# Earlier x slabs, a constant tile for the dummy matmuls, and one product moved from GpSimd to VectorE

## The chip, the cores and the metric

The kernel runs on one core of a Trainium2 chip. The metric is the device time of that core in microseconds (us), the median of several executions; most executions of one kernel agree within 0.3%. Engines are named as in the profile: PE (TensorE matmul), PEld (its weight load), DVE (VectorE), ACT (ScalarE), POOL (GpSimd), SP (SyncE, which issues most transfers here).

Each run sets a kernel against the kernel before, on the same chip and in the same rounds. A ratio is the mean time of the one kernel's fast runs over the mean of the other's fast runs of the same rounds, so it is not quite the ratio of the medians quoted beside it; the bracket after it is a 95% interval.

## The reference, cut to what matters

```python
x  = A_x                                    # 2048 x 640, bf16
xn = layernorm(x)
s  = irfft2(rfft2(xn) * (w_r + 1j*w_i))     # spectral branch
h  = gelu(xn @ w_gate) * (xn @ w_up)        # 640 -> 1536
g  = silu(h @ w_down)                       # 1536 -> 640
return x + s * g
```

## The kernel before

x is held as 16 slabs of 128 x 640. The first two gate/up tiles ("early") multiply **raw** x, so that the PE needn't wait for the layernorm. Their outputs are corrected later on VectorE: out = (raw + wsum * b) * a, where the rows a and b of all four slabs go through DRAM once and come back broadcast as RB. The layernorm statistics of a slab are made on VectorE or on ScalarE in two passes. Normalized slabs are transposed for gate and up, and pairs of them are folded and sent through a small matmul ("fold") for the spectral branch, copied out of PSUM, and stored to DRAM from buffers `mc`.

All work is a list of tasks; a small planner inside the kernel orders each engine's instructions from estimated costs and ranks. Any change of a cost or a rank may therefore reorder everything. Buffers are rings: `mc` has two, `th` two, `ge` three.

```python
    BUFS = dict(sp=2, pg=2, pu=2, s1=4, ma=2, mb=2, mc=2, ..., ge=3, th=2, ...)
    ...
    load_w(Wg, gv, g_in, 0, 2, land=4690)       # slab 0 is issued from ScalarE before this
    load_x(1, 2, land=5200)
    load_w(Wu, uv, u_in, 0, 2, land=6790)
    load_x(2, 3, land=7280)
    load_x(3, 4, land=7750)
    ...
    # stats on ScalarE: its scratch tile is of the ring "th"
    nc.scalar.activation(out=place(junk, (D,)), in_=x, func=ACT.Copy, ...)
    ...
    # the rows a, b: also in a "th" buffer, held until they are stored to DRAM
    sr, rt = Slot("sp"), Slot("th")
    ...
    rs = dma(D5, lambda: rt.tile[0:8, :], (0, -5, 0), 4096, ...)
    rb_in = dma(RB..., D5...partition_broadcast(P), (0, -5, 1), 524288, after=[rs])
    ...
    # the correction of an early tile; k = 0 gate, 1 up
    out = copy of PSUM to ev
    m = scalar_tensor_tensor(ev = RB[:, 1] * WSUM + ev)      # VectorE
    normed.append(... tensor_tensor(ev = ev * RB[:, 0]) on ("POOL" if k else "DVE"))
```

Of the kernel before, what the change touches and what calls it, by code (L numbers as in the profile page):

```python
# [12 lines left out]
BF16 = mybir.dt.bfloat16  # L13
ACT = mybir.ActivationFunctionType
ALU = mybir.AluOpType
P = 128
# [98 lines left out]
class Plan:  # L115
# [12 lines left out]
    def add(self, emit, eng, cost, rank, after=(), new=(), use=(), size=0, slow=1.0, hold=0, order=(), lag=0, land=0):  # L128
        engs = eng if isinstance(eng, dict) else {eng: cost}
        t = Task(emit=emit, engs=engs, rank=rank, after=list(after), new=list(new), size=size, slow=slow, hold=hold, order=list(order), lag=lag, land=land,  # L130
                 seq=len(self.tasks))
        for s in (*new, *use):
            s.users.append(t)
        self.tasks.append(t)
        return t
# [77 lines left out]
def c_act(n, psum=True, extra=0):  # L213
    return 0.833 * n + 60 + extra, 0.833 * n + 200 + extra
# [8 lines left out]
def kernel(  # L223
# [64 lines left out]
    def place(slot, shape, dt=BF16):  # L288
        if slot.tag in ("sp", "pg", "pu"):
            slot.tile = psum.tile([P, *shape], dt, tag=slot.tag, name=slot.tag)  # L290
        else:
            slot.tile = work.tile([P, *shape], dt, tag=slot.tag, name=slot.tag, bufs=BUFS[slot.tag])
        return slot.tile
# [22 lines left out]
    def load_x(a, b, land=0):  # L316
        seq[0] += 1
        t = dma(X[:, a:b, :], xv[:, a:b, :], (0, -4, seq[0]), (b - a) * 163840, use=[sX], land=land)
        for n in range(a, b):
            x_in[n] = t  # L320
# [9 lines left out]
    def load_w(sb, view, got, a, b, land=0):  # L330
        cs = slice(a * P, b * P)
        seq[0] += 1
        w = dma(sb[:, :, cs], view[:, :, cs], (0, -4, seq[0]), (b - a) * 163840, slow=1.1, land=land)
        for t in range(a, b):
            got[t] = w
# [19 lines left out]
    nc.scalar.activation(out=warm, in_=warm, func=ACT.Gelu_apprx_tanh)  # L355
    for w in WF:
        nc.gpsimd.memset(w[:, :, :, L:LP], 0.0)
    idle, heat = Slot("uT"), Slot("sp")

    def blank(e):  # L360
        nc.vector.memset(place(idle, (512,)), 0.0)

    def keep_warm(n, after, rank=(0, -9), ns=425):
        def go(e):
            if heat.tile is None:
                place(heat, (2, 512))
            for k in range(n):
                nc.tensor.matmul(heat.tile[:, k % 2, :], lhsT=idle.tile[:, 0:P], rhs=idle.tile,
                                 start=True, stop=True, skip_group_check=True)
        return add(go, "PE", (n * ns, n * ns), rank, after=after, new=[] if heat.users else [heat], use=[idle] + ([heat] if heat.users else []))  # L370
    seq[0] += 1
    x_in[0] = add(lambda e: None, "SP", (1, 1), (0, -5), size=1, land=3620)
    load_w(Wg, gv, g_in, 0, 2, land=4690)
    load_x(1, 2, land=5200)
    load_w(Wu, uv, u_in, 0, 2, land=6790)
    load_x(2, 3, land=7280)
    load_x(3, 4, land=7750)
    t = add(blank, "DVE", (330, 400), (0, -9), new=[idle])
    t = warmed = keep_warm(6, [t])
    load_gu(2, 4)  # L380
    load_x(4, 6)
    load_tab("f1")
# [71 lines left out]
    def turn_raw(n1):  # L454
        pt = Slot("sp")

        def half():
            return pt.tile[:, 0, :].bitcast(BF16)[:, 0:D]

        def mm(e):  # L460
            place(pt, (2, 512))
            for c in range(5):
                nc.tensor.transpose(out=half()[:, c * P:c * P + P], in_=X[:, n1, c * P:c * P + P], identity=ident)
        a = add(mm, "PE", c_pe(*[140] * 5), (0, n1), after=[x_in[n1], warmed], new=[pt], use=[sX])
        if n1 == 0:
            keep_warm(2, [a], (0, 0, 0))
        raw[n1] = add(lambda e: copy_on(e, XR[:, :, n1 * P + (n1 > 0):(n1 + 1) * P + (n1 > 0)], half().rearrange("p (c n) -> p c n", c=5)),
                      {"ACT": c_act(640)} if n1 < 2 else {"ACT": c_act(640), "DVE": (415, 560)}, None, (0, n1), after=[a], use=[pt], hold={1: 1000}.get(n1, 200))
    for n1 in range(4):
        turn_raw(n1)  # L470

# [68 lines left out]
            outs.append(add(cp, either(640), None, (1, 2 * j + s), after=[a] + outs, new=[] if s else [A], use=[pa, A] if s else [pa]))  # L540
        stored[j] = dma(lambda: D2[:, 2 * j:2 * j + 2, :], lambda: A.tile, (0, -1, j), 327680, after=outs, use=[A], slow=1.1)

    lead = ("DVE", "ACT", "DVE", "ACT")
    for n1 in range(NSLAB):
        if n1 % 2 == 0:
            xn_of[n1 // 2] = Slot("s1")
# [325 lines left out]
    def gate_up(grp, t):  # L872
        pg, pu, ge, u = Slot("pg"), Slot("pu"), Slot("ge"), Slot("uT")
        uT[grp, t] = u
        last = {}
        early = grp == 0 and t < 2
        for k, (w, ps, wt) in enumerate(((Wg, pg, g_in[t]), (Wu, pu, u_in[t]))):
            parts = [(128 * j, 128 * j + 128) for j in range(4)] if grp == 0 and t < 3 else [(0, 512)]
            mm = []
            for lo, hi in parts:  # L880
                def go(e, w=w, ps=ps, lo=lo, hi=hi):
                    if lo == 0:
                        place(ps, (512,))
                    for c in range(5):
                        more = early and lo == 0
                        nc.tensor.matmul(ps.tile[:, lo:hi + more], lhsT=w[:, c, t * P:(t + 1) * P],  # L886
                                         rhs=XR[:, c, lo + (lo > 0):hi + 1 if lo or more else hi] if early else xnT[:, c, grp * 512 + lo:grp * 512 + hi], start=(c == 0), stop=(c == 4),
                                         skip_group_check=True)
                step[0] += 1
                rk = (1, step[0]) if len(parts) == 1 else (0, 5, lo, k, t) if early else (1, lo // 128, t)  # L890
                got = raw if early else turned
                mm.append(add(go, "PE", c_pe(*[hi - lo] * 5), rk,
                              after=[wt] + mm[-2:] + [got[n] for n in range((grp * 512 + lo) // P, (grp * 512 + hi) // P)],
                              new=[ps] if lo == 0 else [], use=[] if lo == 0 else [ps]))
                if early and lo == 0:
                    sums_out[k, t] = add(lambda e, k=k, ps=ps: copy_on(e, WSUM[:, 2 * k + t:2 * k + t + 1], ps.tile[:, 128:129]),
                                         {"DVE": c_dve(1, 1, True)}, None, (0, -1), after=[mm[-1]], use=[ps])
                    mm.append(sums_out[k, t])
            last[id(w)] = mm[-1]

        def act(e, src=None):
            place(ge, (512,))
            nc.scalar.activation(out=ge.tile, in_=pg.tile if src is None else src, func=ACT.Gelu_apprx_tanh)  # L903

        def mul(e, src=None):
            place(u, (512,))
            nc.vector.tensor_tensor(out=u.tile, in0=pu.tile if src is None else src, in1=ge.tile, op=ALU.mult)  # L907
        if not early:
            a = add(act, "ACT", c_act(512), (0, step[0]), after=[last[id(Wg)]], new=[ge], use=[pg])
            u_done[grp, t] = add(mul, "DVE", c_dve(512, 1, True), (0, step[0]), after=[a, last[id(Wu)]], new=[u], use=[pu, ge])  # L910
            return
        normed, evs = [], []

        def four(s):
            return s.tile.rearrange("p (n t) -> p n t", n=4)
        for k, (w, ps) in enumerate(((Wg, pg), (Wu, pu))):
            ev = Slot(("IU", "R")[k])
            evs.append(ev)
            out = add(lambda e, ev=ev, ps=ps: copy_on(e, place(ev, (512,), FP32), ps.tile), {"ACT": c_act(512), "DVE": c_dve(512, 1, True)}, None, (1, 3, 0.5), after=[last[id(w)]], new=[ev], use=[ps])
            m = add(lambda e, ev=ev, k=k: nc.vector.scalar_tensor_tensor(out=four(ev), in0=RB[:, 1], scalar=WSUM[:, 2 * k + t:2 * k + t + 1], in1=four(ev),  # L920
                                                                         op0=ALU.mult, op1=ALU.add), "DVE", c_dve(512, 1), (0, 100), after=[out, rb_in, sums_out[k, t]], use=[ev])
            normed.append(add(lambda e, ev=ev: (nc.gpsimd if e == "POOL" else nc.vector).tensor_tensor(out=four(ev), in0=four(ev), in1=RB[:, 0], op=ALU.mult), *(("POOL", (1700, 1800), (1, 8)) if k else ("DVE", c_dve(512, 1), (0, 100))), after=[m], use=[ev]))
        a = add(lambda e: act(e, evs[0].tile), "ACT", c_act(512), (0, 100), after=normed[:1], new=[ge], use=evs[:1])
        u_done[grp, t] = add(lambda e: mul(e, evs[1].tile), "DVE", c_dve(512, 1), (0, 100), after=[a, normed[1]], new=[u], use=[ge, evs[1]])

# [127 lines left out]
```

## Time and profile before

| what | before |
|---|---|
| median of the first 3 runs | 202.65 us (202.62 to 202.78) |
| span of the profiled execution | 201.1 us |
| first gate matmul | 5.59 us |
| first gate matmul of 512 columns | 14.23 us |
| start of the last matmul group | 196.34 us |
| from there to the end | 4.74 us |

The first table of the page (engine, busy us, share of the span, instructions):

```profile
PE 195.2 (97%) x1527; PEld 117.4 (58%) x1527; DVE 149.7 (74%) x320; ACT 127.2 (63%) x224; POOL 33.1 (16%) x73
```

The PE is the bound, and the prediction below reads its stages, waits (what waited <- for what: us in all, times, longest) and head. The first is from the list of waits (what waited <- for what: us in all, times, longest), the second from the timeline of VectorE (start, length, instruction, idle time before it):

```profile
ACT mc L296 <- DMA D<-mc: 1.0, 1, 1.0
```

```profile
29.71 0.75 DVE L920 SCALAR_TENSOR_TENSOR IU<-RB,WSUM,IU 128x512 f32<-128x512 f32 x1 [1.12 <-DMA RB<-D]
```

ScalarE waits once, for 1.0 us, until a fold buffer `mc` has been stored. And the corrections start at 29.71, not when the PE or VectorE is ready, but when the rows RB are back from DRAM.

### The profile page before, as it was taken

The page shows a single profiled execution, that of the slowest core. Times are in us where ns is not written, and L with a number is a line of the kernel's source. Part 1 is how long each engine was busy: PE and PEld are TensorE (multiplying, and loading weights), DVE is VectorE, ACT ScalarE, POOL GpSimd, SP SyncE. Part 2 cuts the span into 40 slices and gives each one's busy share as a digit, 9 for nine tenths or more (in the row PEclk, how much of TensorE's full clock was granted, in tenths as well). Part 3 has the DMA queues.
Part 4 walks back from the last instruction along what each step waited for, and adds up shares of the span by engine and source line. Part 5 has one row for each costly group of instructions (what it writes and reads, how often), then busy time and mean ns, then how long its engine had stood idle before and what let it go on. Part 6 is the DMA issues. An engine that isn't in the chain of part 4 may idle for free.

```text
span 201.1 us, 4125 instructions
## 1 busy us (share of the span) xinstructions
PE 195.2 (97%) x1527; PEld 117.4 (58%) x1527; DVE 149.7 (74%) x320; ACT 127.2 (63%) x224; POOL 33.1 (16%) x73
## 2 busy tenths in 40 slices
PE   7999999999999999999999999999999999999992
PEld 2994444566544555677755555467765555457781
DVE  3789969999323249999998999933257788887774
ACT  3898997974632768778775766333466565766421
POOL 2412347596000000000000000000004122211210
PEclk9999999999999999999999999999999999999999
DMA  6999999569949677333244210117704332332432
GB/s 175 329 316 325 344 392 235 126 165 196 301 128 375 223 202 178 103 93 115 61 126 126 75 50 16 68 49 221 317 3 135 96 132 100 98 107 92 130 103 65
DMA packets 35894, 32.62 MB, mean 162 GB/s; under 512 B 10910, under 2 KB 32930, under 8 KB 35874
## 3 DMA queue, kind: packets, MB, share of 16 engines
q1 hardware_dynamic: 34434, 29.49, 49.1%
q0 software_dynamic: 1152, 2.66, 4.8%
q10 hardware_dynamic: 288, 0.20, 0.5%
q8 instruction: 12, 0.20, 0.4%
q14 instruction: 8, 0.07, 0.1%
HBM read 22.51 MB, written 9.19 MB: 158 GB/s over the span
## 4 chain that ended last, share of the span: by engine, by line
PE 79%; DMA 10%; SPq 4%; DVE 3%; issue 1%; ACT 1%; DVEq 0%
PE pg L886 19%; PE pu L886 19%; PE pg L970 13%; PE pu L970 12%; DMA X<-in_A_x_dram 6%; SPq L303 4%; DMA RB<-D 4%; PE sp L697 3%; PE sp L830 3%; PE sp L772 2%; PE sp L806 2%; PE sp L670 2%; PE sp L532 1%; PE sp L690 1%; PE sp L824 1%
## 5 line engine op out<-in xcount | busy, mean ns | idle before, releaser
L886 PE MATMUL pu<-xnT,Wu 128*128 128x512 bf16 (+1 forms) x245 | 57.6, 366 | 0.0
L886 PE MATMUL pg<-xnT,Wg 128*128 128x512 bf16 (+1 forms) x245 | 57.5, 366 | 0.0
L907 DVE TENSOR_TENSOR uT<-pu,ge 128x512 bf16<-128x512 f32 x46 | 31.7, 689 | 20.9 <-PE pu L886 18.4
L970 PEld LDWEIGHTS <-uT 128*128 128x128 bf16 x396 | 37.8, 98 | 14.1 <-issue 0.6
L903 ACT ACTIVATE ge<-pg 128x512 bf16<-128x512 f32 x46 | 27.4, 597 | 25.5 <-PE pg L886 25.0
L886 PEld LDWEIGHTS <-Wg 128*128 128x128 bf16 x285 | 25.2, 98 | 22.1
L886 PEld LDWEIGHTS <-Wu 128*128 128x128 bf16 x285 | 25.1, 98 | 21.8
L970 PE MATMUL pg<-Wd,uT 128*128 128x320 bf16 (+2 forms) x204 | 30.5, 293 | 0.4 <-ACT ge L903 0.4
L970 PE MATMUL pu<-Wd,uT 128*128 128x320 bf16 (+1 forms) x192 | 29.7, 297 | 0.0
L296 ACT CAST ma<-sp 128x644 bf16<-128x644 f32 (+1 forms) x32 | 23.4, 792 | 9.7 <-PE sp L830 7.9
L932 POOL COPY xr<-s 1x1 bf16<-1x1 bf16 x1 | 0.2, 182 | 101.8 <-DVE s L856 101.8
L933 POOL DMA_DIRECT2D xr<-in_A_x_dram x16 | 8.8, 552 | 32.3 <-DVE res L957 31.7
L296 ACT CAST IU<-sp 128x640 bf16<-128x640 f32 x16 | 10.9, 691 | 4.2 <-PE sp L772 4.1
L979 ACT ACTIVATE th<-pg 128x320 f32<-128x320 f32 (+2 forms) x17 | 7.3, 427 | 9.9 <-PE pg L970 8.9
L296 ACT CAST Vt<-sp 128x640 bf16<-128x640 f32 x16 | 10.8, 691 | 3.7 <-PE sp L806 3.7
L984 DVE SCALAR_TENSOR_TENSOR G<-th,pg 128x320 bf16<-128x320 f32 (+1 forms) x16 | 7.7, 479 | 7.1 <-ACT th L979 6.9
L979 ACT ACTIVATE th<-pu 128x320 f32<-128x320 f32 (+1 forms) x16 | 7.0, 438 | 9.2 <-PE pu L970 9.0
L984 DVE SCALAR_TENSOR_TENSOR G<-th,pu 128x320 bf16<-128x320 f32 (+1 forms) x16 | 7.7, 480 | 5.6 <-ACT th L979 5.3
L296 ACT CAST mc<-sp 128x640 bf16<-128x640 f32 x15 | 9.8, 694 | 2.3 <-PE sp L533 1.3
L433 POOL TENSOR_TENSOR RSTD<-MVA,mh 128x1 f32<-128x1 f32 x12 | 8.4, 697 | 4.5 <-DVE MVA L415 3.7
L848 DVE TENSOR_TENSOR mb<-ma 128x640 bf16<-128x640 bf16 x8 | 3.9, 493 | 6.9 <-ACT ma L296 6.9
L750 DVE TENSOR_TENSOR R<-Y 64x644 bf16<-64x644 bf16 x16 | 7.8, 490 | 0.4
(107 smaller groups left out, 252.9 us busy)
## 6 DMA issues: line engine op xcount, KB each, us to landing
BU<-D SPq DMA_DIRECT2D x8, 640.0 KB
D<-mc SPq DMA_DIRECT2D x8, 320.0 KB
D<-IU SPq DMA_DIRECT2D x8, 320.0 KB
xr<-in_A_x_dram POOLq DMA_DIRECT2D x16, 160.0 KB, 2.6
out_dram<-res SPq DMA_DIRECT2D x15, 160.0 KB
Wg<-in_B_w_gate_dram SPq DMA_DIRECT2D x6, 320.0 KB
Wu<-in_B_w_up_dram SPq DMA_DIRECT2D x6, 320.0 KB
Wd<-in_B_w_down_dram SPq DMA_DIRECT2D x6, 320.0 KB
```

What stands on the lines that cost most here:

```text
L296: return nc.scalar.copy(out=out, in_=in_) if e == "ACT" else nc.vector.tensor_copy(out=out, in_=in_)
L303: return add(lambda e: nc.sync.dma_start(out=out() if callable(out) else out, in_=in_() if callable(in_) else in_), "SP", (430, 430), rank ...
L433: nc.gpsimd.tensor_tensor(out=rstd, in0=var, in1=mh, op=ALU.pow)
L697: nc.tensor.matmul(into(q, ri), lhsT=sZ.tile[:, q, ri, :], rhs=FM[:, kinds[q][2] + (4 if ri and kind == 0 else 0), :], start=False, stop=T ...
L750: nc.vector.tensor_tensor(out=o, in0=Yf[:, ::-3, :], in1=Yf[:, 1:3, :], op=ALU.subtract)
L886: nc.tensor.matmul(ps.tile[:, lo:hi + more], lhsT=w[:, c, t * P:(t + 1) * P], rhs=XR[:, c, lo + (lo > 0):hi + 1 if lo or more else hi] if ...
L903: nc.scalar.activation(out=ge.tile, in_=pg.tile if src is None else src, func=ACT.Gelu_apprx_tanh)
L907: nc.vector.tensor_tensor(out=u.tile, in0=pu.tile if src is None else src, in1=ge.tile, op=ALU.mult)
L933: nc.gpsimd.dma_start(out=sx.tile, in_=xv[:, n1, :])
L970: nc.tensor.matmul(ps.tile[:, 0:hi - lo], lhsT=uT[grp, ks[i]].tile[:, j * P:(j + 1) * P], rhs=Wd[:, ks[i], lo:hi], start=(i == 0), stop=(i ...
L979: nc.scalar.activation(out=th.tile[:, 0:hi - lo], in_=ps.tile[:, 0:hi - lo], func=ACT.Tanh, scale=0.5)
L984: nc.vector.scalar_tensor_tensor(out=G2.tile[:, lo:hi], in0=th.tile[:, 0:hi - lo], scalar=1.0, in1=ps.tile[:, 0:hi - lo], op0=ALU.add, op1 ...
```

## The change

Its intent: begin the real PE work sooner (slab 1 ahead of the gate weights, slab 2 ahead of the up weights; dummy matmuls on a constant tile, which need no memset), and take the slow GpSimd product out of the up corrections. The choice of statistics engines for slabs 0 to 3 is changed to go with it. The core of the diff, cut:

```diff
-    load_w(Wg, gv, g_in, 0, 2, land=4690)
-    load_x(1, 2, land=5200)
-    load_w(Wu, uv, u_in, 0, 2, land=6790)
-    load_x(2, 3, land=7280)
-    load_x(3, 4, land=7750)
-    t = add(blank, "DVE", (330, 400), (0, -9), new=[idle])
-    t = warmed = keep_warm(6, [t])
+    load_x(1, 2, land=4150)
+    load_w(Wg, gv, g_in, 0, 2, land=5210)
+    load_x(2, 3, land=5700)
+    load_w(Wu, uv, u_in, 0, 2, land=6760)
+    load_x(3, 4, land=7250)
+    t = warmed = keep_warm(7, [], ns=425)     # lhsT, rhs: a constant tile of ones
 ...
-        if n1 == 0:
-            keep_warm(2, [a], (0, 0, 0))
 ...                                           # raw copies out of PSUM:
-  {"ACT": c_act(640)} if n1 < 2 else {"ACT": ..., "DVE": ...}, hold={1: 1000}
+  {"ACT": c_act(640)} if n1 < 1 else {"ACT": ..., "DVE": ...}, hold={0: 1000, 1: 1000}
 ...
-    lead = ("DVE", "ACT", "DVE", "ACT")
+    lead = ('DVE', 'DVE', 'ACT', 'DVE')
 ...                                           # last product of a correction:
-  *(("POOL", (1700, 1800), (1, 8)) if k else ("DVE", c_dve(512, 1), (0, 100)))
+  "DVE", c_dve(512, 1), (0, 100)
```

More of the change, by code (lines that the diff above doesn't have):

```diff
@@ L357 @@
         nc.gpsimd.memset(w[:, :, :, L:LP], 0.0)
-    idle, heat = Slot("uT"), Slot("sp")
-    def blank(e):
-        nc.vector.memset(place(idle, (512,)), 0.0)
+    heat = Slot("sp")
+    ones = nc.const_aps.tensor(1.0, [P, 512], BF16)
     def keep_warm(n, after, rank=(0, -9), ns=425):
@@ L367, in go @@
             for k in range(n):
-                nc.tensor.matmul(heat.tile[:, k % 2, :], lhsT=idle.tile[:, 0:P], rhs=idle.tile,
+                nc.tensor.matmul(heat.tile[:, k % 2, :], lhsT=ones[:, 0:P], rhs=ones,
                                  start=True, stop=True, skip_group_check=True)
-        return add(go, "PE", (n * ns, n * ns), rank, after=after, new=[] if heat.users else [heat], use=[idle] + ([heat] if heat.users else []))
+        return add(go, "PE", (n * ns, n * ns), rank, after=after, new=[] if heat.users else [heat], use=[heat] if heat.users else [])
     seq[0] += 1
     x_in[0] = add(lambda e: None, "SP", (1, 1), (0, -5), size=1, land=3620)
-    load_w(Wg, gv, g_in, 0, 2, land=4690)
-    load_x(1, 2, land=5200)
-    load_w(Wu, uv, u_in, 0, 2, land=6790)
-    load_x(2, 3, land=7280)
-    load_x(3, 4, land=7750)
-    t = add(blank, "DVE", (330, 400), (0, -9), new=[idle])
-    t = warmed = keep_warm(6, [t])
+    load_x(1, 2, land=4150)
[4 more added lines that the diff above has]
+    t = warmed = keep_warm(7, [], ns=425)
     load_gu(2, 4)
@@ L464, in turn_raw @@
         a = add(mm, "PE", c_pe(*[140] * 5), (0, n1), after=[x_in[n1], warmed], new=[pt], use=[sX])
-        if n1 == 0:
-            keep_warm(2, [a], (0, 0, 0))
         raw[n1] = add(lambda e: copy_on(e, XR[:, :, n1 * P + (n1 > 0):(n1 + 1) * P + (n1 > 0)], half().rearrange("p (c n) -> p c n", c=5)),
-                      {"ACT": c_act(640)} if n1 < 2 else {"ACT": c_act(640), "DVE": (415, 560)}, None, (0, n1), after=[a], use=[pt], hold={1: 1000}.get(n1, 200))
+                      {"ACT": c_act(640)} if n1 < 1 else {"ACT": c_act(640), "DVE": (415, 560)}, None, (0, n1), after=[a], use=[pt], hold={0: 1000, 1: 1000}.get(n1, 200))
     for n1 in range(4):
@@ L921, in gate_up @@
                                                                          op0=ALU.mult, op1=ALU.add), "DVE", c_dve(512, 1), (0, 100), after=[out, rb_in, sums_out[k, t]], use=[ev])
-            normed.append(add(lambda e, ev=ev: (nc.gpsimd if e == "POOL" else nc.vector).tensor_tensor(out=four(ev), in0=four(ev), in1=RB[:, 0], op=ALU.mult), *(("POOL", (1700, 1800), (1, 8)) if k else ("DVE", c_dve(512, 1), (0, 100))), after=[m], use=[ev]))
+            normed.append(add(lambda e, ev=ev: nc.vector.tensor_tensor(out=four(ev), in0=four(ev), in1=RB[:, 0], op=ALU.mult), "DVE", c_dve(512, 1), (0, 100), after=[m], use=[ev]))
         a = add(lambda e: act(e, evs[0].tile), "ACT", c_act(512), (0, 100), after=normed[:1], new=[ge], use=evs[:1])
```

## The prediction

> **What bounds the kernel now.** I read the table of engines first (PE, the TensorE, is busy for 195.2 of 201.1 us), then a table of engine time by stretch, because an average over the whole span can hide a stage with another limit. Columns: stretch, its length, then busy us and instruction count of each engine, the granted PE clock, DMA share, GB/s.
>
> ```profile
> 0.00:5.30 5.30, 3.69 (x13) 1.39 (x13) 1.58 (x6) 2.18 (x3) 1.45 (x14) 1.00 0.68 182
> 5.30:14.20 8.90, 8.89 (x156) 8.81 (x157) 7.05 (x22) 8.19 (x18) 2.87 (x8) 1.00 1.13 325
> 14.20:35.30 21.10, 21.10 (x107) 9.77 (x105) 19.08 (x43) 18.49 (x40) 9.18 (x17) 1.00 1.14 322
> 35.30:51.30 16.00, 15.62 (x114) 10.51 (x113) 15.70 (x36) 11.72 (x26) 10.59 (x19) 1.00 0.74 170
> 51.30:147.00 95.70, 95.70 (x723) 56.45 (x725) 65.77 (x125) 56.27 (x87) 0.00 (x0) 1.00 0.46 145
> 147.00:196.50 49.50, 49.50 (x418) 29.98 (x418) 38.64 (x83) 29.65 (x50) 9.00 (x17) 1.00 0.32 101
> ```
>
> From 5.30 us on the PE is the first figure after the length, and it equals the length in every stretch but one: 15.62 of 16.00. So everything between 5.30 and about 196.5 us is bound by PE work in a fixed order, and only three things can shorten the kernel: starting that work sooner, removing the 0.38 us hole, or shortening the tail from the last matmul's end (about 197.2) to 201.1. The change doesn't touch the tail. The list of PE waits confirms that there is nothing else:
>
> ```profile
> PE sp L368 <- DVE uT L361: 1.2, 1, 1.2
> PE sp L463 <- DMA X<-in_A_x_dram: 0.4, 1, 0.4
> PE pg L970 <- ACT ge L903: 0.4, 1, 0.4
> ```
>
> Then the PE's timeline of the head (start, length, instruction; in brackets the idle time before it). PE lengths overlap because matmuls are pipelined; the distance from start to start is what one costs.
>
> ```profile
> 3.75 0.72 PE L463 MATMUL sp<-ident,X 128*128 128x128 bf16 x5
> 4.28 0.62 PE L368 MATMUL sp<-uT 128*128 128x512 bf16 x2
> 5.30 0.45 PE L463 MATMUL sp<-ident,X 128*128 128x128 bf16 x5 [0.41 <-DMA X<-in_A_x_dram]
> 5.59 0.73 PE L886 MATMUL pg<-XR,Wg 128*128 128x129 bf16 x10
> ```
>
> The reader is to see: slab 0 of x is transposed at 3.75, two dummy matmuls fill in, slab 1 arrives only at 5.30, its five transposes cost 5.59 - 5.30 = 0.29 us, and only then does the first gate matmul run. Gate weights were already there, as the gate ran with no wait of its own.
>
> Last, the VectorE and GpSimd lines around the one hole (37.49 us):
>
> ```profile
> 31.58 0.74 DVE L920 SCALAR_TENSOR_TENSOR R<-RB,WSUM,R 128x512 f32<-128x512 f32 x1
> 32.40 1.27 POOL L922 TENSOR_TENSOR R<-R,RB 128x512 f32<-128x512 f32 x1 [1.26 <-DVE R L920]
> 32.84 1.38 DVE L920 SCALAR_TENSOR_TENSOR IU<-RB,WSUM,IU 128x512 f32<-128x512 f32 x1
> 35.26 1.36 POOL L922 TENSOR_TENSOR R<-R,RB 128x512 f32<-128x512 f32 x1
> 36.01 1.16 DVE L907 TENSOR_TENSOR uT<-R,ge 128x512 bf16<-128x512 f32 x1
> 36.87 0.57 ACT L903 ACTIVATE ge<-pg 128x512 bf16<-128x512 f32 x1
> 37.49 0.97 PE L970 MATMUL pg<-Wd,uT 128*128 128x320 bf16 x6 [0.38 <-ACT ge L903]
> ```
>
> The PE at 37.49 wants a pg PSUM bank that the last gelu of this token group (36.87) must free. That gelu needs one of three ge buffers, and one was held for the first corrected tile until its product at 36.01, which comes late. Both DVE operations that ran beside a POOL product are stretched: the same correction takes 1.38 us instead of 0.75, the same product 1.16 instead of 0.67.
>
> **What the Trainium skill says.** *SBUF — State Buffer*, section "Who interferes with whom": a VectorE instruction with two SBUF inputs contends with a GpSimd instruction that reads SBUF. The 1.38 against 0.75 and 1.16 against 0.67 us agree. *GPSIMD Engine Reference*, section "Engine selection": two-input elementwise work belongs on VectorE, GpSimd being about 2x slower; here 1.27 and 1.36 against 0.68 us for the identical product on DVE, which agrees. *DMA: Bandwidth & Descriptors*, section "Issuing engines are not separate DMA queues": transfers from different issuers share the same 16 engines and interleave. So what counts is bytes ahead of a transfer, and that is how I treat the head below; the trace is consistent (slab 1, second on its queue behind the gate weights at 1.24 us, lands at 5.30), but no run yet shows it by itself. *TensorE: Matmul & The Clock Gate*, section "What's actually happening": the PE runs at half clock until it has been busy for about 3.4 us. The dummies show it: six from 1.21 us take about 0.43 us each, the pair at 4.28 only 0.62 together, so full clock came at about 4.28.
>
> **The change part by part.**
>
> *Load order.* Before: slab 0, gate weights, slab 1, up weights, slab 2, slab 3. After: slab 0 and slab 1, gate weights, slab 2, up weights, slab 3. The first gate matmul needs slab 0 and gate weights. Before, slab 0 (160 KB), gate weights (320 KB) and slab 1 (160 KB) were all in by 5.30. After, the same 640 KB is ahead of the gate, in another order, so the gate weights land at about 5.3 (estimate), while slab 1 is in at about 4.2 and is transposed in what was dummy and idle time. The evacuation of slab 0 ended at 5.19, so it is no later limit. The gate therefore starts at about 5.30 instead of 5.59: **-0.29 us**. Up weights were first used at 6.82 with no wait; slab 2 now goes before them, so they land later by its 160 KB, but the PE then holds gate matmuls of slabs 0 and 1 (two times 0.56 us start to start), slab 2's transposes (0.29) and the first normalized slab's transposes (0.29): 5.30 + 1.70 = 7.0 us, which covers an arrival at about 6.8. Worth 0, with a small risk.
>
> *Constant tile.* The dummies no longer wait for a memset (the first 1.21 us) and can start at about 0.75, when the other queues start. Seven instead of six at 0.43 each is 3.0 us, so they end at about 3.75, just when slab 0 landed (3.72 by VectorE's first read). The last two dummies (0.62 us at 4.28) go. All of it lay in time in which the PE had no data: worth 0, except that the clock must still be up when the gate starts. Activity begins earlier, so I expect full clock by about 4.3 as now.
>
> *Statistics.* Slabs 1 and 3 go from ScalarE to VectorE, slab 2 the other way: one slab more on VectorE, two halves of 0.45 plus 0.21 + 0.15 = +1.26 us; ScalarE loses 0.74 + 0.19 + 0.83 + 0.19 = 1.95; GpSimd loses one 0.19. Slab 1's evacuation may now also be on VectorE (about +0.5 there, -0.7 on ScalarE). VectorE was busy for 7.05 of 8.90 us in that stretch, so it gets nearly full, ScalarE (8.19) gets room. Neither is the path if normalized slabs still come before the raw gate work runs out.
>
> *The last product.* Two POOL products (1.27 + 1.36) go; VectorE gets two at 0.68 = +1.36 us, and gets back the stretching: (1.38 - 0.75) + (1.16 - 0.67) = 1.12. Net only +0.24 us on VectorE, and each correction chain is 0.6 us shorter. The hole needs to shrink by 0.38 us plus the slip next to it (the matmuls at 36.14 should have been followed 0.81 later, at 36.95, not 37.49: 0.54 start to start). I count **-0.40 us** as the mean of full removal (-0.54) and part of it.
>
> *New waits*, all small: **+0.05 us**. Sum: -0.29 - 0.40 + 0.05 = -0.64; 202.65 - 0.64 = **202.0 us**.
>
> **Rivals.** (1) *The head's gain is lost to VectorE.* The third up/gate tile needs all four normalized slabs; before, the last was evacuated at about 13.3 and used at 13.67, so only 0.3 us of slack. If three statistics on VectorE delay it, the PE waits there and 0.3 us is given back, or more. Against: ScalarE's two-pass statistics take 1.95 us a slab and VectorE's 1.26. Result about 202.4 to 202.9. (2) *The clock rises late*, since only transposes follow the seven dummies: early work at half speed for up to 1 us; about 203. Against: the present kernel reached full clock with 2.6 us of dummies and 0.5 us of transposes. (3) *The hole moves.* Instructions are placed by a planner, so every later order may shift; VectorE is at 15.70 of 16.00 us in 35.3 to 51.3, and its spill could make PSUM banks wait or delay the spectral chain. For a long delay there is filler: the PE has gate and down work until 182 us, and the last inverse output is ready at 192.07, some 4 us before its use. Result 202.1 to 202.6. (4) *Everything clicks*: head -0.35, the hole -0.54 and the slip after it: 201.6.
>
> **Range and chances.** The possible gain is bounded: all PE idle that the change can reach is below 1.2 us (0.6% of the time), and nothing but PE work could be lost to more than a microsecond or so. The time should lie in 201.2 to 202.9 with 80%. A 2% step is 4.05 us, far outside both ways: faster 0.01, same 0.98, slower 0.01.
>
> **What would show it.** Right: first gate matmul at about 5.3 with slab 1's transposes before it; no wait for ge at the start of the down products; no POOL instruction at the product's line, four DVE ones at about 0.68, and no stretched DVE neighbours; PE idle after 5.3 of near 0. Wrong: a PE wait for a normalized slab or up weights between 5.3 and 14; dummy-like 0.107 us spacing of 128-column matmuls after 5.3; a new PE wait after 35 us or one longer than 0.5; a longer tail.

## The result, and the profile after

After: **202.67 us** (median of 4, 202.34 to 203.03); before, in the same rounds: 202.72 (202.62 to 202.83). Ratio 0.9998 [0.998, 1.0016]: the same. The prediction's range holds the result, but of the 0.64 us that it expected, 0.05 came. The profiled executions span 200.9 against 201.1 us.

The landmarks after: first gate matmul 5.49, first of 512 columns 14.21, start of the last group 196.01, and 4.89 us from there to the end. Engine totals, and the first three stages from 5.30 us on (stretch, length, then busy time of PE, PEld, DVE, ACT, POOL, granted clock, DMA share, GB/s):

```profile
PE 194.5 (97%) x1508; PEld 117.7 (59%) x1526; DVE 148.6 (74%) x321; ACT 127.0 (63%) x224; POOL 32.4 (16%) x71
```

```profile
5.30:14.20 8.90, 8.70 (x151) 8.51 (x151) 7.78 (x26) 8.32 (x18) 3.33 (x8) 1.00 1.12 326
14.20:35.30 21.10, 20.72 (x104) 9.58 (x104) 18.82 (x44) 18.90 (x42) 6.80 (x14) 1.00 1.15 315
35.30:51.30 16.00, 15.95 (x116) 10.91 (x115) 14.48 (x33) 11.56 (x26) 12.04 (x20) 1.00 0.97 213
```

The loss that used to be in the third of these (15.62 of 16.00) has gone, and one has appeared in the second: 20.72 of 21.10, where it was 21.10 of 21.10. (Matmul records that are missing from the trace lower such sums too, by about 0.05 us each: from 51.30 to 147.00, not shown, the trace gives 95.17 of 95.70 and no wait.) The list of waits says what for:

```profile
ACT mc L296 <- DMA D<-mc: 2.3, 2, 1.2
ACT th L416 <- DMA D<-th: 1.7, 1, 1.7
PE sp L367 <- PEq L1033: 0.8, 1, 0.8
PE sp L528 <- DVE mb L515: 0.3, 1, 0.3
PE pg L882 <- ACT XR L296: 0.3, 1, 0.3
```

The wait for `ge` is no longer there. In its place the PE waits for a fold input (L528), and ScalarE, which had 1.0 us of such waits, has 4.0 us of them for buffers that are still being **stored to DRAM**. The head in the PE's timeline:

```profile
4.00 1.22 PE L461 MATMUL sp<-ident,X 128*128 128x128 bf16 x10
5.49 0.73 PE L882 MATMUL pg<-XR,Wg 128*128 128x129 bf16 x10 [0.27 <-ACT XR L296]
6.06 0.44 PE L461 MATMUL sp<-ident,X 128*128 128x128 bf16 x5
6.34 0.73 PE L882 MATMUL pg<-XR,Wg 128*128 128x128 bf16 x10
7.08 0.74 PE L882 MATMUL pu<-XR,Wu 128*128 128x129 bf16 x10
```

and the timelines of the weight loads, ScalarE and VectorE beside it:

```profile
4.93 0.15 PEld L882 LDWEIGHTS <-Wg 128*128 128x128 bf16 x1
...
7.07 0.17 PEld L882 LDWEIGHTS <-Wu 128*128 128x128 bf16 x3 [0.18 <-DMA Wu<-in_B_w_up_dram]
```

```profile
4.75 1.29 ACT L296 COPY XR<-sp 128x640 bf16<-128x640 bf16 x2 [2.09 <-PE sp L461]
```

```profile
3.98 0.89 DVE L409 BATCH_NORM_STATS2 STAT<-X 128x6 f32<-128x320 bf16 x2 [3.12 <-DMA X<-in_A_x_dram]
```

Slab 1 is transposed together with slab 0, as intended. But slab 0 itself is first read at 3.98, where it was 3.72; its copy out of PSUM starts at 4.75 instead of 4.50, and the gate matmul waits for that copy, while a gate weight was already loaded at 4.93. Then the up weights come late: 6.34 to 7.08 is 0.74 us for ten matmuls which take 0.57 elsewhere, 0.17 lost.

The new hole in the PE's timeline, then the lines of VectorE, ScalarE and SyncE's queue that lead to it:

```profile
28.79 1.24 PE L882 MATMUL pg<-xnT,Wg 128*128 128x512 bf16 x5
30.31 0.39 PE L528 MATMUL sp<-mb,F1T 128*128 128x512 bf16 x1 [0.28 <-DVE mb L515]
```

```profile
28.01 0.45 DVE L445 TENSOR_SCALAR s<-X,NM,RSTD 128x640 bf16<-128x640 bf16 x1 [0.45 <-POOL RSTD L431]
...
29.77 0.48 DVE L515 TENSOR_TENSOR mb<-ma 128x640 bf16<-128x640 bf16 x1
```

```profile
22.19 0.74 ACT L416 ACTIVATE th<-X 128x640 bf16<-128x640 bf16 x1 [1.68 <-DMA D<-th]
```

```profile
16.97 0.35 SPq L303 DMA_DIRECT2D D<-th  x1
```

Read from the bottom: the 4 KB store of the rows a and b is issued at 16.97; its `th` buffer is free for ScalarE's statistics only at 22.19, after 1.68 us of idling; ScalarE works without a pause from there to the statistics of the next slab, and that normalized slab comes late (28.01, after 0.45 us of waiting for its root, the reciprocal standard deviation); its fold ends at 30.25; the PE runs it at 30.31. From start to start 1.52 us pass where 1.08 would do: **0.44 us**. In the kernel before, ScalarE's third such operation after 13 us came at 22.22 and didn't wait; in its order the fourth pair of folds comes only at 38.44, not at 30.31. In the roomy kernel below, which has no wait for `th`, it starts at 20.46.

### The profile page after: what moved, and what is told of

Read it like the earlier page. It is cut to its first block, busy times and chain, and to the rows that moved or that the text cites. A ratio compares the mean times of both kernels' runs of the same rounds, so it can differ in the third digit from the quotient of the medians.

```text
span 200.9 us, 4104 instructions
## 1 busy us (share of the span) xinstructions
PE 194.5 (97%) x1508; PEld 117.7 (59%) x1526; DVE 148.6 (74%) x321; ACT 127.0 (63%) x224; POOL 32.4 (16%) x71
## 4 chain that ended last, share of the span: by engine, by line
PE 82%; DMA 6%; SPq 4%; DVE 2%; issue 2%; ACT 2%; POOL 1%; DVEq 0%
PE pu L882 21%; PE pg L882 20%; PE pg L966 13%; PE pu L966 13%; DMA X<-in_A_x_dram 6%; SPq L303 4%; PE sp L693 3%; PE sp L826 3%; PE sp L768 2%; PE sp L802 2%; PE sp L666 2%; PE sp L528 1%; PE sp L686 1%; PE sp L820 1%; ACT th L419 1%
## 5 line engine op out<-in xcount | busy, mean ns | idle before, releaser
L882 PE MATMUL pu<-xnT,Wu 128*128 128x512 bf16 (+1 forms) x238 | 57.0, 365 | 0.4
L882 PE MATMUL pg<-xnT,Wg 128*128 128x512 bf16 (+1 forms) x234 | 56.5, 365 | 0.5
L296 ACT CAST mc<-sp 128x640 bf16<-128x640 f32 x16 | 10.8, 696 | 3.5 <-DMA D<-mc 2.3
L409 DVE BATCH_NORM_STATS2 STAT<-X 128x6 f32<-128x320 bf16 x12 | 5.5, 483 | 4.0 <-DMA X<-in_A_x_dram 4.0
L416 ACT ACTIVATE th<-X 128x640 bf16<-128x640 bf16 x10 | 7.4, 745 | 1.7 <-DMA D<-th 1.7
```

The costliest lines, as they stand in the source:

```text
L296: return nc.scalar.copy(out=out, in_=in_) if e == "ACT" else nc.vector.tensor_copy(out=out, in_=in_)
L882: nc.tensor.matmul(ps.tile[:, lo:hi + more], lhsT=w[:, c, t * P:(t + 1) * P], rhs=XR[:, c, lo + (lo > 0):hi + 1 if lo or more else hi] if ...
```

## The experiments

Twelve kernels ran, each against the kernel before in five rounds; all results were correct. Two kinds have to be told apart. An **a_** or **b_** kernel keeps the instruction order of after or before (except where said) and changes one thing in it. A **p_** kernel puts one part of the change into before and lets the planner order anew.

### The changed kernel once more, unedited

> The changed kernel once more, unedited, to see how its times and spans scatter. Both theories: 202.3 to 203.0 us, as in its first four runs (the kernel before scatters by 0.2 only). In the profile the PE hole at about 30.3 us (0.28 idle, waiting for the last fold product on VectorE) and the ScalarE idle of 1.7 us before 22.2 us should come back, if they belong to the kernel and not to one execution.

Measured: 203.15 us (202.28 to 203.64) against 202.86, ratio 1.0006 [0.9986, 1.0027]. Its six executions scatter over 1.36 us, those of before over 0.58. PE timeline and ScalarE waits of the profiled one:

```profile
50.41 0.38 PE L528 MATMUL sp<-mb,F1T 128*128 128x512 bf16 x1 [0.27 <-ACT mc L296]
...
51.01 0.38 PE L528 MATMUL sp<-mb,F1T 128*128 128x512 bf16 x1 [0.16 <-ACT mc L296]
```

```profile
ACT mc L296 <- DMA D<-mc: 3.9, 3, 1.9
...
ACT th L416 <- DMA D<-th: 1.3, 1, 1.3
```

The hole at 30.31 isn't there; two others are, 20 us later, behind stores of `mc`. So **the holes move from execution to execution**, which a single trace can't show. Its head lost more too: slab 2's transposes and the up weights each about 0.2 us late, so that 14.21 became 14.49.

### The rows a and b outside the th ring

```diff
-... out=place(rt, (P,), FP32)[0:8, :]
+... out=own(rt)[0:8, :]       # own: 256 columns of the table TI, which is loaded later
```

> The changed kernel with the transposed statistics rows in storage of their own (a table that is loaded much later), so that no ScalarE statistic has to wait until those rows have been stored to DRAM; the order of instructions on every engine is unchanged. Ring theory (the new PE hole comes from ScalarE, which waits 1.68 us for a th buffer): ScalarE idle before 22.2 us is gone, the fold is earlier, the PE hole at 30.3 is gone, time 0.3 to 0.5 us below the changed kernel, about 202.2. Rival (VectorE is overfull because of the statistics and the two products that it took over): ScalarE's idle goes but the hole stays and the time is the same within 0.15 us.

Measured: 202.83 us (202.29 to 203.38) against 202.86, 0.9999 [0.9984, 1.0013]. ScalarE's wait for `th` and the 0.28 us hole are gone, but in its timeline there is now:

```profile
28.16 0.69 ACT L296 CAST mc<-sp 128x640 bf16<-128x640 f32 x1 [2.31 <-DMA D<-mc]
```

ScalarE waits 5.4 us in all for `mc` stores, and the PE slips 0.1 to 0.2 us at a time at single fold matmuls (one at 30.31, where the roomy kernel below has it at 30.20; the next one 1.04 us after the down matmuls at 39.23, which take 0.81), too little for the list of waits. From its first 512-column gate to its last group it takes 181.80 us, as long as after. One ring freed, the next one waits: half of the theory stood.

### The old engine in the new order, and the new engine in the old order

```diff
 a_pool, in after:   (nc.gpsimd if k else nc.vector).tensor_tensor(...)   # planned as before on "DVE"
 b_dve,  in before:  nc.vector.tensor_tensor(...)                         # planned as before on "POOL"
```

> The changed kernel in its unchanged order with the two products back on GpSimd. If the move of the products itself is what removed the old hole: stretched VectorE neighbours (1.4 and 1.2 us) come back, one PE wait of 0.3 to 0.6 us appears between 36 and 41 us, time +0.3 to +0.6 over the changed kernel. Rival (the old hole went because the new order puts the last gelu ahead): stretched neighbours come back but no PE wait over 0.15 us, time within 0.15 us of the changed kernel.

> The kernel before in its unchanged order with the two products on VectorE. Prediction's step: no stretched neighbours, hole at 37.5 gone, time -0.4 us, about 202.3. Rival (the products stand in VectorE's order ahead of the one that frees the ge buffer): the freeing product ends at about 37.2 instead of 36.85, the hole grows to 0.4 to 0.9 us, time 0 to +0.4.

Measured: a_pool 203.12 us (202.38 to 203.51), 1.0005 [0.9989, 1.002]; b_dve 202.94 (202.89 to 203.05), 1.0003 [0.9991, 1.0015]; before 202.86. First a_pool: VectorE, GpSimd, PE.

```profile
33.49 1.16 DVE L918 TENSOR_TENSOR IU<-IU,RB 128x512 f32<-128x512 f32 x1
```

```profile
32.39 1.72 POOL L918 TENSOR_TENSOR R<-R,RB 128x512 f32<-128x512 f32 x1 [2.20 <-DVE R L916]
```

```profile
36.92 0.98 PE L966 MATMUL pu<-Wd,uT 128*128 128x320 bf16 x6
37.73 0.98 PE L966 MATMUL pg<-Wd,uT 128*128 128x320 bf16 x6
```

With the product on GpSimd a VectorE neighbour is stretched again (1.16 against 0.68 us), yet the down products follow each other without a hole. Then b_dve, VectorE and PE:

```profile
29.65 0.75 DVE L920 SCALAR_TENSOR_TENSOR IU<-RB,WSUM,IU 128x512 f32<-128x512 f32 x1 [1.10 <-DMA RB<-D]
...
36.50 0.69 DVE L907 TENSOR_TENSOR uT<-R,ge 128x512 bf16<-128x512 f32 x1
```

```profile
37.40 0.97 PE L970 MATMUL pg<-Wd,uT 128*128 128x320 bf16 x6 [0.36 <-ACT ge L903]
```

Nothing is stretched any more, yet the hole stays. VectorE's product that frees the `ge` buffer ends at 36.50 + 0.69 = 37.19, where in before it ended at 36.01 + 1.16 = 37.17: the two products that VectorE took over cost what it got back. So **the order removed the hole, not the engine**. In the new order that product starts at 35.16, and a fourth pair of folds runs on the PE ahead of the down products, which start at 36.26 instead of 35.29.

### Room for the stores: the same order, more buffers

Only storage changes: the rows a and b lie in TI, and odd folds write to parts of XR and TI that are free at that time instead of to the `mc` ring, which so serves every second fold.

```diff
-                if s == 0:
+                if s == 0 and j % 2 == 0:
                     place(A, (2, D))
+                elif s == 0:
+                    A.tile = (flat(XR)[:, 1280 * (j // 4):][:, 0:1280] if j in (3, 5)
+                              else flat(TI)[:, 0:1280]).rearrange("p (s d) -> p s d", s=2)
...
+    own = lambda s: ... flat(TI)[:, 1280:1536].bitcast(FP32)
-    ... out=place(rt, (P,), FP32)[0:8, :]
+    ... out=own(rt)[0:8, :]
```

> The changed kernel, order of work unchanged, with the statistics rows in storage of their own and every second fold output (mc) in storage that is idle then, so that ScalarE's evacuations need not wait for a store to DRAM two folds back. Store theory (the new PE holes of 0.3 to 0.8 us at the fold matmuls, in another place in each execution, come from ScalarE waiting for th and mc buffers whose stores have not landed): no ScalarE wait on a store, no PE wait over 0.1 us after 8 us, time 0.3 to 0.6 below the changed kernel's of the same rounds, about 202.3 to 202.5. Rival (the folds are late for VectorE's sake): ScalarE's waits go, PE holes at fold matmuls stay, waiting for a fold product on VectorE; time within 0.15.

Measured: 202.42 us (202.24 to 202.68) against 202.88, **0.9979 [0.9964, 0.9993]**. All waits of the PE (the first is the launch):

```profile
PE sp L367 <- PEq L1035: 0.8, 1, 0.8
PE pg L884 <- ACT XR L296: 0.2, 1, 0.2
PE sp L461 <- DMA X<-in_A_x_dram: 0.2, 1, 0.2
```

ScalarE has no wait for a store left, the PE none in the list after the head, and the scatter fell from 1.36 us (six executions of after) to 0.44 (four of this). The three kernels of the last section, built on this one, have medians of 202.28, 202.57 and 202.26. The last group of matmuls, in before and then here:

```profile
196.34 0.83 PE L970 MATMUL pg<-Wd,uT 128*128 128x128 bf16 x12
```

```profile
195.73 0.83 PE L968 MATMUL pg<-Wd,uT 128*128 128x128 bf16 x12
```

The control puts the same storage into before:

> Control: the kernel before, order unchanged, with the same extra storage for the statistics rows and every second fold output. Theory (the waits for stores delay the PE only in the changed order): ScalarE's 1.0 us of waits on stores go, the hole of 0.4 us at the first down products stays, time within 0.2 of the kernel before. Rival (the storage helps any kernel alike): -0.4 us as for the changed kernel.

Measured: 202.9 us (202.75 to 203.4) against 202.84, 0.9999 [0.9979, 1.0019]. Waits of the PE, and its timeline:

```profile
PE sp L368 <- DVE uT L361: 1.2, 1, 1.2
PE pg L972 <- ACT ge L905: 0.3, 1, 0.3
```

```profile
37.50 0.97 PE L972 MATMUL pg<-Wd,uT 128*128 128x320 bf16 x6 [0.28 <-ACT ge L905]
```

More room alone gives nothing: before doesn't wait for stores in a way that reaches the PE. The new order plus room gains, each alone does not. This is the experiment that settles where the middle's gain went.

b_roomy shows one thing more. Its first 512-column gate matmul came 0.36 us later than in before (14.59, not 14.23), but the matmul after the hole came at 37.50 (before 37.49, b_dve 37.40), and the last group at 196.36 (196.34, 196.37). In these three profiles the hole took up what the head lost: the corrections start when RB lands (29.71, 29.65 and again 29.71), and that doesn't move with the head.

### One part at a time, planned anew

> The kernel before with the load order, constant tile and evacuation choice of the changed one alone (statistics and product as before; the planner orders anew). Theory (the head gains nothing, since slab 0 lands 0.25 later and up weights become the wait): first gate at about 5.5, PE wait for up weights at about 7, the first 512-column gate at 14.2 or later, time 0 to +0.4 over the kernel before, with a scatter of 1 us. Prediction's step: gate at 5.3, time -0.3.

> The kernel before with the statistics of slabs 1 and 3 on VectorE and of slab 2 on ScalarE alone (planned anew). Theory: the head stays bound by loads and PE order, so within 0.2 of the kernel before. Rival (VectorE gets too full): normalized slabs come late, a PE wait between 9 and 14 us, +0.3 or more.

> The kernel before with the products on VectorE alone, planned anew (the run with the old order kept its hole of 0.36 us, as the products stood ahead of the one that frees the ge buffer). If planning anew is what removes the hole: no PE wait over 0.1 us at the first down products, time -0.3 to -0.6. If not: hole stays or another one appears at a fold matmul, time within 0.2.

```diff
 p_loads: load order, constant tile, choice of the raw copies' engine     p_lead: the "lead" line     p_prod: the product's line
```

Measured against 202.88: p_loads **204.59** (204.42 to 205.13), 1.0088 [1.0074, 1.0103]; p_lead 203.44 (203.40 to 203.59), 1.0029 [1.0016, 1.0042]; p_prod 203.0 (202.68 to 204.13), 1.0011 [0.9991, 1.003]. In p_loads, for one, the PE's timeline has a new hole at the down products:

```profile
35.99 0.98 PE L966 MATMUL pg<-Wd,uT 128*128 128x320 bf16 x6
37.35 0.97 PE L966 MATMUL pu<-Wd,uT 128*128 128x320 bf16 x6 [0.39 <-DVE uT L903]
```

p_loads missed both of its forecasts: the gate came at 5.12, earlier than in any other profile, and still the time rose. Of the 1.5 us that its span is longer, 0.86 were lost by the first 512-column gate (15.09). p_lead was 0.6 us slower, as its rival said, but without the wait that the rival gave as the reason: the PE has none between 9 and 14 us. Its first 512-column gate comes at 15.03. The matmuls from 5.27 to 6.84 took 1.57 us for what before did in 0.93 (5.30 to 6.23), of which more below; whether that was so in all its executions isn't known.

By medians, +1.7, +0.6 and +0.1 us add up to +2.4, and together the parts make -0.05. With a planner between change and instruction, parts don't add: each run measures another order. p_prod does agree with the tests above: no hole at the down products, but two small ones (0.22, 0.16) at fold matmuls behind ScalarE's `mc`.

### The head, on top of the roomy kernel

> The changed kernel with the extra storage, and slab 0's evacuation split over ScalarE (three fifths) and VectorE (two fifths), so that the first gate need not wait for it. Arrival theory (the head is bound by the arrival of the up weights at about 7.1): first gate 0.2 earlier, at about 5.25, the PE waits by as much longer for up weights, the first 512-column gate stays at 14.2, time as with the extra storage alone (202.4) within 0.15. Rival (slab 0's evacuation is the bound of the head): first 512-column gate at 14.0, time -0.2.

a_split: VectorE copies 2/5 of slab 0 out of PSUM, ScalarE 3/5, so that the gate is released sooner. Measured: 202.28 us (202.13 to 204.3) against 202.84, 0.9992 [0.9955, 1.0029]. A miss. ScalarE's timeline:

```profile
5.03 0.48 ACT L466 COPY XR<-sp 128x384 bf16<-128x384 bf16 x1 [2.37 <-DVE XR L465]
```

ScalarE's copy waited for VectorE's, so the two ran one after the other and the gate came at 5.56. Two of six executions (203.99, 204.3) were about 1.8 us above the rest for no reason that a trace of ours holds; one of before (203.89) and one of p_prod (204.13) did so too.

> The changed kernel with the extra storage, and up weights loaded ahead of the third slab, planned anew. Arrival theory: up weights in at about 6.8 and no PE wait for them, first 512-column gate 0.1 to 0.2 earlier, time -0.1 to -0.2 against the extra storage alone if the planner's order is otherwise as good. Rival (any new order brings its own holes of some 0.5 us): time +0.2 or more with a PE wait after 14 us.

a_wu_first: up weights ahead of slab 2, planned anew. Measured: 202.57 us (202.25 to 203.04) against 202.84, 0.9979 [0.9959, 0.9999]. The up weights are now wanted sooner and are waited for longer, 0.35 us against 0.18 in after:

```profile
6.44 0.57 PEld L884 LDWEIGHTS <-Wu 128*128 128x128 bf16 x10 [0.35 <-DMA Wu<-in_B_w_up_dram]
```

So the arrival theory missed, and so did its rival: no PE wait came after 14 us.

> The changed kernel with the extra storage and slab 0's evacuation on VectorE instead of ScalarE, order otherwise unchanged (the split over both engines did not do it: the second copy waited for the first). Arrival theory (the head is bound by the arrival of the up weights at about 7.1): first gate 0.15 to 0.25 earlier than 5.5, the PE then waits 0.3 to 0.5 us for up weights, first 512-column gate at 14.1 to 14.2, time that of the extra storage alone (202.4) within 0.15. Rival (slab 0's evacuation is the bound of the head): no wait for up weights over 0.1, first 512-column gate at or before 14.0, time 0.2 lower.

a_evac: slab 0's copy on VectorE (`copy_on(e if n1 else "DVE", ...)`). Measured: **202.26 us** (202.13 to 202.54) against 202.99, **0.9957 [0.9944, 0.9969]**, the best of all, and below both kernels. VectorE and PE:

```profile
4.89 0.47 DVE L296 COPY XR<-sp 128x640 bf16<-128x640 bf16 x1
```

```profile
5.41 1.20 PE L884 MATMUL pg<-XR,Wg 128*128 128x129 bf16 x10
6.44 0.44 PE L461 MATMUL sp<-ident,X 128*128 128x128 bf16 x5
```

The copy takes 0.47 us where ScalarE's took 0.69 in before, and the gate has no wait. It follows slab 0's arrival by 5.41 - 4.08 = 1.33 us (5.49 - 3.98 = 1.51 in after; in both, the transposes of slab 0 ran at the slow early rate that is described below). But this profiled execution had those ten gate matmuls at 1.03 us instead of 0.57, and so it can't say whether the up weights would bound the head once the gate is faster; that stays open. It also ran on another chip than a_roomy and the two intervals touch, so the step from 202.42 to 202.26 is not shown to be more than chance.

## Why the prediction was right or wrong

The class (same) was right. The range, 201.2 to 202.9, holds the result with some luck: six more executions of the same kernel have a median of 203.15, outside it. The sum was wrong: -0.64 expected, -0.05 measured. The landmarks say where it went (us, profiled executions; "middle" is the third column less the second, "tail" the span less the third; spans and tails to two decimals are from the packed traces):

| kernel | gate | first 512-column gate | last group | span | middle | tail |
|---|---|---|---|---|---|---|
| before | 5.59 | 14.23 | 196.34 | 201.09 | 182.11 | 4.74 |
| after | 5.49 | 14.21 | 196.01 | 200.90 | 181.80 | 4.89 |
| after again | 5.53 | 14.49 | 196.63 | 201.52 | 182.14 | 4.89 |
| roomy | 5.63 | 14.27 | 195.73 | 200.63 | 181.46 | 4.89 |

- **The head, -0.29: mis-sized.** In these two profiles the gate came 0.10 us earlier, and by 14.2 us 0.02 was left. The step that failed is "The evacuation of slab 0 ended at 5.19, so it is no later limit": it ended at 4.75 + 0.69 = 5.44 in after, and the gate waited for it. VectorE's first read of slab 0 came at 3.64 to 3.78 us in the five profiles with the old load order, at 3.78 to 4.11 in the nine with the new one. Why it is later isn't shown: slab 1 now travels beside slab 0, but before it the gate weights did, issued at 0.72 as well. The gate weights, expected at about 5.3, were no limit: the first was loaded at 4.93. In p_loads, where slab 0 was read at 3.78, the gate came at 5.12. And the up weights, "Worth 0, with a small risk", cost 0.17.
- **The hole, -0.40: it went, but for another reason.** It is gone in all profiles of the new order, and the middle without other waits (roomy) is 182.11 - 181.46 = 0.65 us shorter than before, more than the 0.54 of full removal; in before the fold after the hole came 0.95 us after the matmuls at 37.49, which take 0.81. But "each correction chain is 0.6 us shorter" is wrong: b_dve shows the chain's end at 37.19 against 37.17. The prediction's own net of +0.24 us on VectorE was the warning, as VectorE was the path there. The stretching was read correctly, and a_pool brought it back.
- **The new waits, +0.05: the step that failed.** The hole at 30.31 cost 0.44 us in the first profile, whose middle is 181.80 - 181.46 = 0.34 us longer than in the roomy kernel; in the second the middle is 182.14 - 181.46 = 0.68 us longer. That is half to all of the 0.65 that the new order gains. The trigger is a ring of two buffers whose release is a store to DRAM: `th` or `mc`. Shown by a_roomy with b_roomy beside it.
- **The rivals.** (3), "The hole moves", is what came, though through ScalarE's buffers and not through VectorE being full as I argued: VectorE went from 15.70 to 14.48 of 16.00 us. (1) didn't come: the PE waits for no normalized slab in after. (2), the late clock, came in some executions of either head: ten gate matmuls at the start took 1.00 (a_pool), 1.03 (a_evac) and 1.09 us (p_lead, old head) instead of 0.57, about 0.45 us lost in 3 of the 14 profiles. Nothing ties it to the change: the 128-column matmuls go from 0.107 to 0.056 us apart at about 4.0 us in p_loads and 6.5 in a_pool (new head), by 4.3 in before and at 6.8 in p_lead (old head). So "full clock by about 4.3 as now" was read from a single execution: the full rate came 3.1 us after the first dummy there and 5.6 us after it in p_lead, where the prediction reckoned with about 3.4. Head landmarks of single profiles can differ by some 0.5 us for this alone: the first 512-column gate came at 14.23, 14.41 and 14.59 in the three profiles with before's order, at 14.10 to 14.50 in the seven with after's. Head differences of 0.1 us in the table are not resolved.
- **Open.** The seven profiles with after's order have a tail of 4.89 to 4.92 us, the three with before's 4.74 to 4.76, with the same instructions. The difference lies behind the issue of the last store (2.65 to 2.68 us to the end against 2.50 to 2.52); none of my runs explains it. Nor do they explain the outliers of 1 to 2 us.

The sum closes for roomy: +0.04 by 14.2, -0.65 in the middle, +0.15 in the tail make -0.46, which is 201.09 to 200.63 by span, and its median is 202.88 - 202.42 = 0.46 below that of before.

## What to carry to other kernels

Here a buffer whose release was a store to DRAM was a hidden wait: it cost nothing until a reorder brought its next user forward, and 0.34 to 0.68 us then. So look at the waits of engines that are not the bound before you predict what a new order gives. Where a planner stands between an edit and the instructions, test the engine and the order apart (new engine in the old order, old engine in the new), as single parts planned anew don't add up. And read holes from more than one execution: here the same kernel had its hole at 30 us once and at 50 us the next time.

## What the Trainium skill lacked or had wrong

- *Perfetto Trace Analysis*, section "Optimization Strategy", takes consistent bubbles, the same gap repeating on the engine that should be saturated, as a possible sign of too few buffers. Here the bubbles were not consistent (0.28 us at 30.31 in one execution, 0.27 and 0.16 us at 50.41 and 51.01 in another of the same kernel) and buffers were still the cause: with more of them the PE had no wait after the head. A wait that a DMA releases should be named as a cause of bubbles that move.
- *DMA: Bandwidth & Descriptors*, section "Anatomy of one DMA — SWDGE (gpsimd) path", gives about 2.0 us as the fixed part of one transfer, for transfers that GpSimd issues. It has no such figure for a small store that SyncE issues among other transfers, and there 2.0 us is not the number to plan with: the 4 KB store issued at 16.97 us gave its `th` buffer back only at 22.19, some 5.2 us, in a stretch where the mean DMA share was 1.15.
- No page has the case in which work moved off GpSimd frees VectorE of contention and loads it by as much: the freeing product ended at 37.17 us before and at 37.19 after the move, in the same order.
